# Attention with a thresholded softmax and a softplus MLP on one core: whole softmax weights for eight units instead of four, the last keys' transposes in the score banks, later sums of value halves, and keys a tile sooner

## The chip, the cores and the metric

The kernel runs on one core of a Trainium2 chip. The metric is its device time in microseconds (us); the time before is the median of three runs. Five engines work side by side, each through its own instructions in order: PE (matmuls; its weight loads show as PEld), DVE, ACT, POOL and SP, which here issues the DMAs.

## The reference

```
scores = (1/8) q k^T                       # 8 batches, 8 heads, 576 rows, 64 wide
scores = where(scores >= max(scores) - tau, scores, -1e9)
attn   = exp(scores - max) / (sum + 1e-9)
x      = (attn v), heads side by side      # 4608 tokens of 512
h      = x @ w_in                          # 512 -> 2048
out    = softplus(h) @ w_out               # 2048 -> 512
```

## The kernel before, in words

**Units and tiles.** A unit is two heads of one batch: 32 units. Each has nine tiles of 128 query rows: four of the first head's first 512 rows, one (tile 4) with the last 64 rows of both heads, four of the second head. The main loop (lines 972 to 1012) runs over 288 tiles and writes the instructions of several stages in each: the maximum and exponentials of the tile two ahead, the mask of the next, the transposes of this one, the scores of the tile three ahead, and MLP matmuls by a quota (`PAT`, one letter a step). Twice a tile `point()` runs what `defer(n, f)` put off by n points.

**A tile.** `scores` (line 443) puts 128 x 576 scores as two halves of 288 columns into one of two score buffers of two PSUM banks each; the rest of each bank is free. `row_max` (DVE, negm), `exps` (ACT, into e_all, then thr) and `mask` (DVE: scores compared with thr, times e_all, row sums kept) follow. The next scores into that buffer wait for the mask.

**Whole and halved weights.** For a unit with `s.whole` (the first `NF`) the fp32 weights are transposed on PE: `whole_T` (line 492) makes four 128 x 128 transposes into a PSUM tile tm and a fifth of 64 columns, the last keys', into another, tr; `whole_copy` lets ACT copy both to SBUF (gw); `whole_values` multiplies with fp32 values in 20 products a unit, and ACT copies the result to xp. For the others `weights_hi` (POOL) and `weights_lo` (DVE) split the weights into two f16 halves e16, a transposing DMA on SP brings them to eT (`weights_T`), values are scaled (ACT) and split in two (POOL, `split_v`, tile vt), and `values` (line 561) makes 36 f16 products a unit. A product then holds both value halves in its partitions; `values_out` copies one half to xp on ACT and adds the other on DVE.

**Keys and queries.** `load` fetches k and q of the unit after next (SP), `split_k` and `split_q` split them on POOL, `qkT` transposes them on PE, ACT copies them out, and two DMAs (`swap`, lines 425 and 426) exchange the partition halves of the queries, since scores need both arrangements. `ST` gives the tile of the unit before at which each of these eight steps stands (`pre`, line 895; `extras`, line 907), `VO` the tiles at which the four products of halved values stand, counted on into the next unit.

**The MLP.** Chunks of 512 tokens: `hidden` (line 677), softplus on ACT in pairs with a table load, halves on POOL (g), `project` (line 741). The first chunk starts at tile 42, in unit 4. The weights are prepared by ACT, POOL and DVE in the first some 70 tiles, one piece in two tiles. A last part, after the attention, is the MLP alone. Score buffers apart, all PSUM tiles (h, o, pv, tr, tm, rT, topv) take turns in four banks, ps_g.

**Who sets the order.** Tile's scheduler orders each engine's instructions from the order of writing; from tile 72 on (`TQ`) DVE and ACT keep the order of writing. All of it is fixed before the run.

Of the kernel before, what the change touches and what calls it, by code (L numbers as in the profile page):

```python
# [9 lines left out]
F32 = mybir.dt.float32  # L10
# [4 lines left out]
ALU = mybir.AluOpType  # L15
# [9 lines left out]
P = 128  # L25
# [7 lines left out]
LAG0 = 6  # L33
PAT = "RemhlTfpSfxvwp"
WD = 4
ST = (1, 3, 4, 4, 5, 6, 6, 8)
VO = (7, 8, 11, 12)
RT = 1
Q9 = (0.9, 1.1, 0.9, 1.1, 1.1, 0.8, 1.2, 0.6, 1.1)
WS2 = 2  # L40
LT = 4
WB = 3
NW = 33
NF = 4
NX = 5
TE = 84
VW = (2, 5, 7, 9)
# [14 lines left out]
def tile_kernel(ctx: ExitStack, tc: tile.TileContext, q, k, v, tau, w_in, w_out, out):  # L62
# [13 lines left out]
    SR = S - SM  # L76
    HS = S // 2
    NC = SM // P
# [12 lines left out]
    ps_g = ctx.enter_context(tc.tile_pool(name="ps_g", bufs=GB, space=PSUM))  # L91
# [66 lines left out]
    vec = Queue(nc.vector)  # L158
# [148 lines left out]
    units = []  # L307
    for b in range(B):
        for hp in range(NPAIR):
            s = Unit()  # L310
            s.i, s.b, s.hp = len(units), b, hp
            s.whole = s.i < NF
            s.r_d = dpool.tile([9, P], F32, name=f"r_d{s.i}")
            units.append(s)

    def load(s):
        h0 = 2 * s.hp
        s.kn = apool.tile([P, 10, D], F32, tag="nat", bufs=2, name=f"kn_{s.i}")
        s.qn = apool.tile([P, 10, D], F32, tag="nat", bufs=2, name=f"qn_{s.i}")
        for t, src in ((s.kn, k), (s.qn, q)):  # L320
            load_rows(s, t, src)
            for j in range(2):
                nc.sync.dma_start(t[j * SR:(j + 1) * SR, NC, :], src[s.b, h0 + j, SM:S, :])
# [119 lines left out]
    def scores(s, t):  # L443
        if t == 0:
            s.sums = apool.tile([P, 9], F32, tag="sums", name=f"sums_{s.i}")
            s.e, s.sp, s.m, s.e16, s.eT = {}, {}, {}, {}, {}
        sp = banks[nth[0] % SB]
        s.e[t] = e_all[:, nth[0] % EB, :]
        nth[0] += 1
        s.sp[t] = sp  # L450
        if t == M:
            parts = [(qm[:, n, j, :], j) for j in range(2) for n in range(2)]
        else:
            j, c = divmod(t, NC + 1)
            parts = [(s.qT[j][n][:, c * P:(c + 1) * P], j) for n in range(2)]
        for m, (lhs, j) in enumerate(parts):
            for hf in range(2):
                nc.tensor.matmul(sp[:, hf, 0:HS], lhs, s.kT[j][:, hf * HS:(hf + 1) * HS],  # L458
                                 start=(m == 0), stop=(m == len(parts) - 1))
# [32 lines left out]
    def whole_T(s, t):  # L492
        e = s.e.pop(t)
        main = ps_g.tile([P, NC, P], F32, tag="g", name=f"tm_{s.i}_{t}")
        rest = ps_g.tile([P, NC, P], F32, tag="g", name=f"tr_{s.i}_{t}")[0:SR, 0, :]
        for c in range(NC):
            nc.tensor.transpose(main[:, c, :], e[:, SR + c * P:SR + (c + 1) * P], ident)
        nc.tensor.transpose(rest, e[:, 0:SR], ident)
        s.e16[t] = main, rest
# [61 lines left out]
    def values(s, g):  # L561
        if g == 0:
            s.xp = apool.tile([P, S], F32, tag="xp", bufs=NX, name=f"xp_{s.i}")
        j, x0 = g // 2, g % 2 * HS
        o = ps_g.tile([P, 512], F32, tag="g", name=f"pv_{s.i}_{g}")
        for c in range(9):
            slot = 0 if c == 0 else 1 + 4 * ((c - 1) % 2) + (c - 1) // 2
            nc.tensor.matmul(o[:, 0:HS], s.vt[:, j, slot, :], s.eT[j][:, c, x0:x0 + HS], start=(c == 0), stop=(c == 8))  # L568
        defer(1, lambda: values_out(s, g, o))

    def values_out(s, g, o):
        j, x0, n = g // 2, g % 2 * HS, HS
        keep = slice(j * D, (j + 1) * D)
        move = slice((1 - j) * D, (2 - j) * D)
        xs = s.xp[keep, x0:x0 + n]
        act.copy(xs, o[move, 0:n])
        vec.tensor_tensor(out=xs, in0=o[keep, 0:n], in1=xs, op=ALU.add)

    def row_scales(s):
        s.rs = apool.tile([P, 9], F32, tag="rs", name=f"rs_{s.i}")  # L580
        if s.whole:
            vec.tensor_scalar(out=s.rs, in0=s.sums, scalar1=1e-9, scalar2=None, op0=ALU.add)
        else:
            vec.tensor_scalar(out=s.rs, in0=s.sums, scalar1=1e-9, scalar2=v_scale[:, s.i:s.i + 1],
                              op0=ALU.add, op1=ALU.mult)
        vec.reciprocal(s.rs, s.rs)

    def row_scales_T(s):
        ps = ps_g.tile([P, 512], F32, tag="g", name=f"rT_{s.i}")
        nc.tensor.transpose(ps[0:9, 0:P], s.rs, ident)  # L590
        defer(1, lambda: row_scales_out(s, ps))
# [255 lines left out]
    def defer(n, f):  # L847
        if n == 0:
            f()
        else:  # L850
            later.append((now["p"] + n, f))
# [38 lines left out]
    for kind, g in WL:  # L890
        for m in range(4):
            n = len(prep)
            prep.append((int(W0 + n * W1), prep_w, (kind, g, m)))

    def pre(s, first_):

        def a():
            split_k(s)
        def b():
            split_q(s, 0)  # L900
            qkT(s, 0, 0)
        def d():
            split_q(s, 1)
        return [a, b, lambda: qkT(s, 0, 2), lambda: qkT(s, 0, 1), d, lambda: qkT(s, 1, 0), lambda: qkT(s, 1, 1),
                lambda: qkT(s, 1, 2)]

    def extras(i, t):

        cur = units[i]
        nxt = units[i + 1] if i + 1 < len(units) else None  # L910
        prev = units[i - 1] if i else None
        for s, t_ in ((prev, t + 9), (cur, t)):
            if s and t_ in (VW if s.whole else VO):
                (whole_values if s.whole else values)(s, (VW if s.whole else VO).index(t_))
        if t == RT and prev:
            row_scales_T(prev)
        if t == 8:
            row_scales(cur)
        if nxt:
            if t == 0:  # L920
                cur.nxt = pre(nxt, False)
            for n, f in enumerate(cur.nxt):
                if ST[n] == t:
                    f()
        for f in plan.pop((i, t), ()):
            f()
        if t == 8 and i + 2 < len(units):
            load(units[i + 2])

    plan = {}  # L930
# [26 lines left out]
    for n in (0, 2, 1):  # L957
        qkT(u0, 1, n)
        point()
    u0.eng, u0.eng_lo = eng, nc.gpsimd  # L960
    scores(*tiles[0])
    row_max(*tiles[0])
    exps(*tiles[0])
    scores(*tiles[1])
    row_max(*tiles[1])
    exps(*tiles[1])
    mask(*tiles[0])
    scores(*tiles[2])
    load_v(units[1])

    done = 0.0
    for g, (cur, t) in enumerate(tiles):
# [7 lines left out]
        for step in PAT:  # L980
            if step == "T":
                if cur.whole:
                    whole_T(cur, t)
                    whole_copy(cur, t)
                else:
                    weights_T(cur, t)
            elif step == "h" and nxt and not nxt[0].whole:
                weights_hi(*nxt)
            elif step == "l" and not cur.whole:
                weights_lo(cur, t)  # L990
            elif step == "R" and ahead:
                row_max(*ahead)
            elif step == "e" and ahead:
                exps(*ahead)
            elif step == "m" and nxt:
                mask(*nxt)
            elif step == "f":
                upto += quota / PAT.count("f")
                while done < upto:
                    done += next(ffn)  # L1000
            elif step == "x":
                extras(cur.i, t)
            elif step == "S" and g + 3 < NS:
                scores(*tiles[g + 3])
            elif step == "v":
                slow_products()
            elif step == "w":
                while prep and prep[0][0] <= g:
                    _, f, a = prep.pop(0)
                    f(*a)  # L1010
            elif step == "p":
                point()

    last = units[-1]
    rest = {15: lambda: row_scales_T(last), 21: lambda: values(last, 2), 24: lambda: values(last, 3)}
# [36 lines left out]
```

## Time and profile before

| | |
|---|---|
| runs, median (lowest to highest) | 1436.69 us (1435.36 to 1439.61) |
| the profiled execution, its time | 1435.47 us |
| its span in the trace | 1433.2 us |
| mean granted clock of PE | 0.967 |
| PE busy | 1267.3 us (88%), 6996 matmuls |
| POOL busy | 1010.3 us (70%) |
| DVE busy | 948.6 us (66%) |
| ACT busy | 901.3 us (63%) |

Busy times are sums of instructions' durations; a busy PE overlaps the end of one matmul with the next, so its sum is no measure of its pace. A group of the profile reads: line, engine, operation, output<-input, shapes, count, then busy time and mean ns of one, then the engine's idle time just before them and what ended it. Most DVE and ACT work has line 151, a helper's, so its groups are told apart by names. A row of the waits reads: who waited <- for whom: us in all, times, longest.

### The profile page before, as it was taken

How to read it: one execution, taken by the hardware profiler on the slowest of the kernel's cores; microseconds unless marked ns; L12 is line 12 of the kernel's file. 1: busy time of each engine (PE TensorE's matmuls, PEld its weight loads, DVE VectorE, ACT ScalarE, POOL GpSimd, SP SyncE). 2: the span in 40 equal slices, each digit the busy share in tenths (PEclk: the TensorE clock that was granted, in tenths of full speed). 3: DMA queues.
4: the chain of work that ended last, by engine and by line, in shares of the span. 5: the costliest groups of instructions: out<-in, count | busy, mean ns of one | idle time of the engine just before them, and what ended most of it. 6: DMA issues, size and time to landing. Idle time of an engine off the chain costs nothing.

```text
span 1433.2 us, 21979 instructions
## 1 busy us (share of the span) xinstructions
PE 1267.3 (88%) x6996; PEld 741.0 (52%) x6996; DVE 948.6 (66%) x1747; ACT 901.3 (63%) x1683; POOL 1010.3 (70%) x1085
## 2 busy tenths in 40 slices
PE   6988477878899989999999999999989899999998
PEld 5555244444555555555555545555555655554455
DVE  6788777876777776778677877777567575651011
ACT  5777475755576658766876677666765658653222
POOL 2678999888777777778777877787766667546242
PEclk9999689989999999999999999999999999999999
DMA  5544566745766676667666666666547545541010
GB/s 152 140 131 114 125 148 152 146 98 114 157 120 132 133 154 131 135 133 156 132 132 130 141 144 128 130 134 157 126 95 155 112 105 107 97 78 39 1 37 15
DMA packets 395074, 170.83 MB, mean 119 GB/s; under 512 B 337072, under 2 KB 374224, under 8 KB 394960
## 3 DMA queue, kind: packets, MB, share of 16 engines
q1 hardware_dynamic: 394960, 169.45, 54.3%
q8 instruction: 55, 0.90, 0.3%
q14 instruction: 59, 0.48, 0.1%
HBM read 63.96 MB, written 10.63 MB: 52 GB/s over the span
## 4 chain that ended last, share of the span: by engine, by line
PE 35%; ACT 20%; DVE 15%; POOL 12%; DMA 8%; issue 7%; SPq 3%; DVEq 0%; ACTq 0%; POOLq 0%
PE o L754 12%; PE h L690 8%; PE s L458 6%; ACT st L151 6%; ACT L151 5%; DVE negm L151 5%; DMA qT<-qT 4%; PE pv L568 4%; ACT e_all L151 3%; DVE e L151 3%; DVE e_all L151 3%; ACT xp L151 2%; PE pv L527 2%; POOL e L541 1%; PE tr L405 1%
## 5 line engine op out<-in xcount | busy, mean ns | idle before, releaser
L754 PE MATMUL o<-w_o,g 128*128 128x512 f16 x1728 | 425.2, 386 | 7.3 <-ACT kT L151 4.8
L690 PE MATMUL h<-xh,w_i 128*128 128x512 f16 (+1 forms) x1280 | 368.2, 363 | 11.7 <-ACT kT L151 6.8
L541 POOL TENSOR_SCALAR e<-e_all 128x576 f16<-128x576 f32 x252 | 229.1, 911 | 159.8 <-DVE e_all L151 155.7
L151 ACT ACTIVATE e_all<-s,negm 128x576 f32<-128x576 f32 x288 | 213.4, 741 | 180.8 <-DVE negm L151 167.9
L458 PE MATMUL s<-kT,qT 128*128 128x288 f32 x1024 | 224.1, 337 | 96.8 <-DVE e_all L151 53.4
L690 PEld LDWEIGHTS <-w_i 128*128 128x128 f16 x1920 | 179.9, 99 | 173.6 <-issue 22.5
L151 DVE TENSOR_REDUCE negm<-s 128x1 f32<-128x576 f32 x288 | 215.8, 750 | 66.0 <-PE s L458 63.6
L754 PEld LDWEIGHTS <-g 128*128 128x128 f16 x1728 | 158.7, 99 | 176.3 <-issue 13.9
L458 PEld LDWEIGHTS s<-kT,qT 128*128 128x128 f32 x1024 | 156.9, 197 | 175.6 <-DVE e_all L151 115.6
L151 DVE SCALAR_TENSOR_TENSOR e_all<-s,thr,e_all 128x576 f32<-128x576 f32 x288 | 232.8, 808 | 20.5 <-ACT thr L151 18.8
L151 DVE SCALAR_TENSOR_TENSOR e<-e_all,e 128x576 f16<-128x576 f32 x252 | 233.5, 926 | 19.5 <-POOL e L541 19.3
L690 PE MATMUL h<-xl,w_i 128*128 128x512 f16 (+1 forms) x640 | 232.0, 363 | 3.6 <-POOL xl L175 3.6
L174 POOL TENSOR_SCALAR g<-st 128x512 f16<-128x512 f32 x144 | 91.6, 638 | 138.1 <-ACT st L151 137.7
L175 POOL TENSOR_TENSOR g<-st,g 128x512 f16<-128x512 f32 x144 | 176.1, 1225 | 9.3
L151 DVE TENSOR_TENSOR xp<-pv,xp 64x288 f32<-64x288 f32 x112 | 50.5, 451 | 184.7 <-ACT xp L151 184.1
L151 DVE SCALAR_TENSOR_TENSOR acc<-o,c,acc 128x512 f32<-128x512 f32 x108 | 80.1, 742 | 132.5 <-PE o L754 71.7
L151 ACT ACT_TABLE_LOAD x119 | 152.7, 1283 | 24.0 <-DVE negm L151 22.3
L568 PE MATMUL pv<-eT,vt 128*128 128x288 f16 x1008 | 151.1, 291 | 0.0
L151 ACT ACTIVATE st<-h,c 128x512 f32<-128x512 f32 x144 | 91.2, 684 | 71.1 <-PE h L690 70.4
L568 PEld LDWEIGHTS <-vt 128*128 128x128 f16 x1008 | 97.0, 100 | 46.6 <-issue 4.2
L151 ACT COPY xp<-pv 64x288 f32<-64x288 f32 (+3 forms) x132 | 50.6, 386 | 92.2 <-PE pv L568 88.3
L151 ACT ACTIVATE st<-st,c 128x512 f32<-128x512 f32 x144 | 96.0, 714 | 2.1
(104 smaller groups left out, 1561.5 us busy)
## 6 DMA issues: line engine op xcount, KB each, us to landing
qT<-qT SPq DMA_DIRECT2D x124, 128.0 KB
vn<-in_v_dram SPq DMA_DIRECT2D x112, 128.0 KB
kn<-in_k_dram SPq DMA_DIRECT2D x32, 256.0 KB
qn<-in_q_dram SPq DMA_DIRECT2D x32, 256.0 KB
wc_i<-in_moe_w_in_dram SPq DMA_DIRECT2D x16, 512.0 KB
R<-r_d SPq DMA_DIRECT2D x64, 128.0 KB
wc_o<-in_moe_w_out_dram SPq DMA_DIRECT2D x16, 512.0 KB
out_dram<-acc SPq DMA_DIRECT2D x32, 256.0 KB
```

What stands on the lines that cost most here:

```text
L151: i = getattr(self.eng, name)(*args, **kwargs)
L174: nc.gpsimd.tensor_scalar(out=hi, in0=x, scalar1=1.0, scalar2=1.0, op0=ALU.mult, op1=ALU.mult)
L175: nc.gpsimd.tensor_tensor(out=lo, in0=x, in1=hi, op=ALU.subtract)
L405: nc.tensor.transpose(pr[:, c * P:(c + 1) * P], src, identr)
L458: nc.tensor.matmul(sp[:, hf, 0:HS], lhs, s.kT[j][:, hf * HS:(hf + 1) * HS], start=(m == 0), stop=(m == len(parts) - 1))
L527: nc.tensor.matmul(o[0:D, 0:n], s.vn[k_, 5 * j + c, :], h[k_, c, 0:n], start=(c == 0), stop=(c == NC))
L541: nc.gpsimd.tensor_scalar(out=h[:, :, 0, :], in0=s.e[t].rearrange("p (c n) -> p c n", n=SR), scalar1=2.0 ** 15, scalar2=1.0, op0=ALU.mult, ...
L568: nc.tensor.matmul(o[:, 0:HS], s.vt[:, j, slot, :], s.eT[j][:, c, x0:x0 + HS], start=(c == 0), stop=(c == 8))
L690: nc.tensor.matmul(bank[:, i * u.T:(i + 1) * u.T], wi[g, cc][:, a, e], x[cc], start=(cc == 0 and m == 0), stop=(cc == NCC - 1 and m == 2))
L754: nc.tensor.matmul(o, u.g[fc][m // 2][:, sl], wo[fc][:, m % 2, :], start=(n == 0), stop=(n == 3 * QF - 1))
```

## The change

- `NF` 4 -> 8: units 4 to 7 keep weights and values whole, as units 0 to 3 do.
- The fifth transpose goes to columns 288 to 415 of the first bank of the score buffer that the same tile's scores were in, not to a PSUM tile of its own; by then that buffer holds the scores of the tile two later.
- The DVE sum of value halves is put off by one point behind ACT's copy.
- `ST`: six of the eight steps that prepare the next unit's keys and queries stand a tile sooner. `VO`: the products of halved values stand a tile sooner. The loads for the unit after next are issued at tile 7 instead of 8.

```diff
-ST = (1, 3, 4, 4, 5, 6, 6, 8)
-VO = (7, 8, 11, 12)
+ST = (0, 2, 3, 3, 4, 5, 6, 8)
+VO = (6, 7, 10, 11)
...
-NF = 4
+NF = 8
...
     def scores(s, t):
...
         s.sp[t] = sp
+        s.bank[t] = sp
...
     def whole_T(s, t):
         e = s.e.pop(t)
         main = ps_g.tile([P, NC, P], F32, tag="g", name=f"tm_{s.i}_{t}")
-        rest = ps_g.tile([P, NC, P], F32, tag="g", name=f"tr_{s.i}_{t}")[0:SR, 0, :]
+        rest = s.bank.pop(t)[0:SR, 0, HS:HS + P]
...
     def values_out(s, g, o):
...
         act.copy(xs, o[move, 0:n])
-        vec.tensor_tensor(out=xs, in0=o[keep, 0:n], in1=xs, op=ALU.add)
+        defer(1, lambda: vec.tensor_tensor(out=xs, in0=o[keep, 0:n], in1=xs, op=ALU.add))
...
     def extras(i, t):
...
-        if t == 8 and i + 2 < len(units):
+        if t == 7 and i + 2 < len(units):
             load(units[i + 2])
```

The change moves instructions on every engine. First PE at the first tiles of unit 1 (tm the four transposes, tr or s_1 the fifth, s_0 and s_1 the two score buffers, pv value products). Before:

```order
L497 MATMUL tm_1_0_564<-identr_81,e_all_129 128x128 x3
L498 MATMUL tr_1_0_565<-identr_81,e_all_129 64x128 [waits Activation_49]
L458 MATMUL s_0_130<-kT_1_0_350,qT0_1_0_389 128x288 [waits DVE_49]
L458 MATMUL s_0_130<-kT_1_0_350,qT0_1_0_389 128x288
L458 MATMUL s_0_130<-kT_1_0_350,qT1_1_0_390 128x288 x2
L527 MATMUL pv_0_3_578<-gw_0_3_500,vn_0_171 64x256 [waits Activation_49]
```

After:

```order
L498 MATMUL tm_1_0_555<-identr_81,e_all_129 128x128 x3
L528 MATMUL pv_0_3_568<-gw_0_3_492,vn_0_171 64x256 [waits Activation_49]
L528 MATMUL pv_0_3_568<-gw_0_3_492,vn_0_171 64x256
L499 MATMUL s_1_131<-identr_81,e_all_129 64x128 [waits Activation_49]
L459 MATMUL s_0_130<-kT_1_0_321,qT0_1_0_356 128x288 [waits DVE_49]
L459 MATMUL s_0_130<-kT_1_0_321,qT0_1_0_356 128x288
L459 MATMUL s_0_130<-kT_1_0_321,qT1_1_0_357 128x288 x2
```

The fifth transpose (line 499) has moved behind value products, into buffer s_1; the ACT instruction that it waits for is the exponentials of tile 2, whose scores are in s_1. In all 72 whole tiles the mask of the tile two later (DVE) waits for ACT's copy of that transpose; before it waited for thr.

Then SP, where the swapped queries of unit 14 are issued (qn_15 the query load of the unit after; qm the last rows' queries, qT the others'; eT a transposing DMA). Before:

```order
L556 DMA_TRANSPOSE eT_13_1_5869<-e16_13_4_5801 128x9x64
L630 DMA xst_6_0_11937<-x_d0_93 128x256
L425 DMA qm_95<-qm_95 64x256
L426 DMA qm_95<-qm_95 64x256
L425 DMA qT1_14_0_5901<-qT0_14_0_5900 64x512
L426 DMA qT1_14_0_5901<-qT0_14_0_5900 64x512
L559 DMA_TRANSPOSE eT_13_1_5869<-e16_13_5_5866 128x9x128
L326 DMA qn_15_6089<-in_q_dram 128x2x256
```

After:

```order
L557 DMA_TRANSPOSE eT_13_1_5891<-e16_13_4_5826 128x9x64
L326 DMA qn_15_6057<-in_q_dram 128x2x256
L425 DMA qm_95<-qm_95 64x256
L426 DMA qm_95<-qm_95 64x256
L425 DMA qT1_14_0_5863<-qT0_14_0_5862 64x512
L426 DMA qT1_14_0_5863<-qT0_14_0_5862 64x512
L323 DMA qn_15_6057<-in_q_dram 64x64 x2
```

The query load, which waits until POOL has split unit 14's second queries, now stands ahead of the swaps; so it is in units 10 to 25.

Last DVE, at the sums of value halves of unit 12 (xp), between the maxima (negm), masks (e_all) and low halves (e16) of unit 13. Before:

```order
L151 TENSOR_TENSOR xp_12_5593<-pv_12_2_5783,xp_12_5593 64x288
L151 TENSOR_REDUCE negm_13_5_5795<-s_0_130 128x1
L151 SCALAR_TENSOR_TENSOR e_all_129,sums_13_5535<-s_1_131,thr_13_4_5754,e_all_129 128x576
L151 SCALAR_TENSOR_TENSOR e16_13_3_5759<-e_all_129,e16_13_3_5759 128x9x64
L151 TENSOR_REDUCE vtop_14_5847<-vn_14_5693 128x1
L151 TENSOR_TENSOR xp_12_5593<-pv_12_3_5828,xp_12_5593 64x288
```

After:

```order
L151 TENSOR_TENSOR xp_12_5561<-pv_12_2_5744,xp_12_5561 64x288
L151 TENSOR_REDUCE negm_13_5_5820<-s_0_130 128x1
L151 SCALAR_TENSOR_TENSOR e_all_129,sums_13_5546<-s_1_131,thr_13_4_5769,e_all_129 128x576
L151 SCALAR_TENSOR_TENSOR e16_13_3_5774<-e_all_129,e16_13_3_5774 128x9x64
L151 TENSOR_TENSOR xp_12_5561<-pv_12_3_5799,xp_12_5561 64x288
L151 TENSOR_REDUCE vtop_14_5864<-vn_14_5700 128x1
```

The adds stand where they stood, or one instruction sooner, while on PE the products they add stand a tile sooner.

More of the change, by code (lines that the diff above doesn't have):

```diff
@@ L445, in scores @@
             s.sums = apool.tile([P, 9], F32, tag="sums", name=f"sums_{s.i}")
-            s.e, s.sp, s.m, s.e16, s.eT = {}, {}, {}, {}, {}
+            s.e, s.sp, s.m, s.e16, s.eT, s.bank = {}, {}, {}, {}, {}, {}
         sp = banks[nth[0] % SB]
```

## The prediction

> **What bounds the kernel now.** I read the page's head first, then one table of stretches cut at the units (a unit is two heads of one batch, nine tiles of 128 query rows), then the waits of PE in two of these stretches. Columns of the table: length, then busy time (x instructions) of PE, PEld, DVE, ACT, POOL, granted clock, DMA share, GB/s.
>
> ```profile
> span 1433.2 us, 21979 instructions
> 13.00:133.20 120.20, 103.28 (x566) 69.34 (x566) 96.74 (x208) 89.23 (x229) 76.14 (x82) 0.96 0.49 137
> 133.20:182.50 49.30, 27.99 (x124) 17.27 (x122) 38.44 (x58) 24.96 (x52) 45.37 (x47) 0.72 0.50 120
> 133.20:334.50 201.30, 144.03 (x715) 83.62 (x714) 156.22 (x268) 120.55 (x221) 178.02 (x185) 0.86 0.59 133
> 334.50:1275.00 940.50, 861.57 (x4875) 503.57 (x4874) 661.38 (x1213) 636.36 (x1143) 688.99 (x735) 0.99 0.62 129
> 412.50:449.40 36.90, 34.39 (x196) 19.73 (x194) 25.80 (x47) 26.90 (x51) 26.25 (x30) 1.00 0.68 132
> 1275.00:1433.20 158.20, 153.07 (x820) 79.97 (x817) 28.65 (x53) 49.84 (x80) 63.81 (x75) 1.00 0.11 29
> ```
>
> There are four stages. Units 0 to 3 (13.0 to 133.2) take 30.1 us each. Units 4 to 7 (133.2 to 334.5) take 50.3 us each with POOL busy 178.0 of 201.3 us and DVE 156.2, while PE does 144.0 at a clock of 0.86: the vector engines bound this stage. From unit 8 on a unit takes 36.9 us (the row at 412.5) and PE is 93% busy at full clock: PE bounds, and each of its waits costs its length. The tail is the MLP alone, at 97% PE; the change doesn't touch it.
>
> Waits of PE, first from 334.5 to 1275, then from 133 to 334.5 (us, times, longest), and between them the longest wait of any engine in the first stretch:
>
> ```profile
> PE s L458 <- DMA qT<-qT: 33.5, 22, 3.5
> PE s L458 <- DVE e_all L151: 21.1, 40, 3.1
> PE tr L405 <- DVE topv L151: 9.1, 12, 0.8
> DVE xp L151 <- ACT xp L151: 180.0, 80, 6.8
> PE s L458 <- DVE e_all L151: 35.6, 20, 9.7
> ```
>
> So in the long stage PE loses 33.5 us where the first scores of the next unit wait for the swapped queries, and 21.1 us where scores wait for a mask. DVE stands 180 us before the sum of value halves, but DVE is only 70% busy there; that wait counts only as far as masks behind it are late.
>
> **Units 4 to 7: what goes.** Groups of the stretch 133.2 to 334.5 alone, by form:
>
> ```profile
> L541 POOL TENSOR_SCALAR e<-e_all 128x576 f16<-128x576 f32 x35 | 30.4, 868 | 6.9 <-DVE e_all L151 6.2
> L151 DVE SCALAR_TENSOR_TENSOR e<-e_all,e 128x576 f16<-128x576 f32 x35 | 38.0, 1087 | 11.0 <-POOL e L541 11.0
> L175 POOL TENSOR_TENSOR vt<-vn,vt 128x576 f16<-128x576 f32 x8 | 11.4, 1422 | 0.5
> L174 POOL TENSOR_SCALAR vt<-vn 128x576 f16<-128x576 f32 x8 | 7.7, 959 | 0.2
> L151 ACT ACTIVATE vn<-vn,v_scale 128x576 f32<-128x576 f32 x8 | 6.2, 771 | 0.0
> L151 DVE TENSOR_TENSOR xp<-pv,xp 64x288 f32<-64x288 f32 x12 | 5.4, 452 | 0.2
> ```
>
> Whole weights need no f16 halves, no split values, no sums of halves. POOL loses 30.4 + 11.4 + 7.7 = 49.5 us of its 178.0; DVE loses 38.0 + 5.4 = 43.4 of 156.2, and the 11.0 it stood waiting for POOL. On SP 40 transposing DMAs and 12 of the 24 value loads go too; nothing in this stage waits on them long, so I count them at nothing.
>
> **Units 4 to 7: what comes.** From units 0 to 3, which already work so: PE's timeline (start, length), beside it nine products of f16 halves in a later unit, and ACT's groups of the whole run:
>
> ```profile
> 84.75 0.66 PE L497 MATMUL tm<-identr,e_all 128*128 128x128 f32 x4
> 85.24 0.27 PE L498 MATMUL tr<-identr,e_all 128*64 128x128 f32 x1
> 85.27 0.54 PE L405 MATMUL tr<-identr,k 128*128 128x128 f32 x4
> 85.74 1.22 PE L527 MATMUL pv<-gw,vn 128*64 128x256 f32 x4
> 86.89 0.80 PE L458 MATMUL s<-kT,qT 128*128 128x288 f32 x4
> 502.80 0.60 PE L754 MATMUL o<-w_o,g 128*128 128x512 f16 x2
> 503.24 1.27 PE L568 MATMUL pv<-eT,vt 128*128 128x288 f16 x9
> 504.35 1.03 PE L754 MATMUL o<-w_o,g 128*128 128x512 f16 x4
> L151 ACT COPY gw<-tm 128x512 f32<-128x512 f32 x32 | 18.6, 582 | 8.1 <-PE tm L497 8.0
> L151 ACT COPY gw<-tr 64x128 f32<-64x128 f32 x32 | 8.4, 263 | 0.0
> ```
>
> Matmuls overlap, so I price them from start to start. Five transposes take 85.27 - 84.75 = 0.52 us, 4.7 a unit. A value product of whole weights takes (86.89 - 85.74) / 4 = 0.29 us, 20 a unit = 5.8; nine of f16 halves take 504.35 - 503.24 = 1.11, four times 4.4. PE gains 4.7 + 5.8 - 4.4 = 6.1 us a unit. ACT gains about 36 x (0.58 + 0.26) = 30 us of copies and loses 6.2 of scaling: 120.6 + 24 = 145. (Value copies stay about as they are.)
>
> With POOL at 128.5 and DVE at 113, PE paces the stage: 36.9 + 6.1 = 43.0 us for units 5 to 7, 129 in all. Unit 4 has MLP work only in its last three tiles; its POOL falls from 45.4 to 33 of 49.3 us, and I put it at 42. That is 171 for 201.3: **-30 us**. The bounds: PE's 144.0 us at the later stage's clock are 144.0 x 0.86 / 0.99 = 125, with the added 24 us 149, and at its 93% 161 us; if ACT, in order and at 145, waits for transposes as long as POOL now works, 196. So -40 to -5.
>
> **The last keys' transposes in score banks (units 0 to 7).** The order shows what this does: before, the fifth transpose of a tile follows its four; now it stands behind the exponentials of the tile two later, whose scores lie in that bank, and the mask of that tile now waits until ACT has copied the transposes out. Transpose and copies become links of the chain scores, maximum, exponentials, mask, next scores. Two tiles of unit 1, ACT and DVE:
>
> ```profile
> 49.99 0.74 ACT L151 ACTIVATE e_all<-s,negm 128x576 f32<-128x576 f32 x1
> 51.51 0.81 DVE L151 SCALAR_TENSOR_TENSOR e_all<-s,thr,e_all 128x576 f32<-128x576 f32 x1
> 54.57 0.74 ACT L151 ACTIVATE e_all<-s,negm 128x576 f32<-128x576 f32 x1
> 57.60 0.81 DVE L151 SCALAR_TENSOR_TENSOR e_all<-s,thr,e_all 128x576 f32<-128x576 f32 x1
> ```
>
> The links are 0.27 + 0.58 + 0.26 = 1.11 us behind the exponentials. In the first tile the mask starts 51.51 - 50.73 = 0.78 us after them, in the second 57.60 - 55.31 = 2.29: the first would be 0.3 late, the second not at all. Fully on the path it costs 1.11 us x 72 = 80, fully hidden nothing; I take 0.25 us a tile, since DVE, busy 97 of 120 us there, has other work to put between: **+18 us**. One PSUM buffer fewer per tile is worth nothing by these rows (no wait of PE for it above).
>
> The Trainium skill speaks against this edit: its page "PSUM — Partial Sum Buffer", section "PSUM bank collisions raise a hardware error", has two engines keep apart by bank and partition quadrant, not by address. Hence the wait, though the columns differ. The trace of before has no such sharing and can't show it.
>
> **Keys a tile sooner.** At one unit's end, on PE:
>
> ```profile
> 515.51 0.53 PE L405 MATMUL tr<-identr,q 128*128 128x128 f32 x4
> ...
> 520.50 0.50 PE L458 MATMUL s<-kT,qT 128*128 128x288 f32 x2
> 520.84 0.23 PE L405 MATMUL tr<-identr,q 128*128 128x128 f32 x1
> 523.09 0.53 PE L458 MATMUL s<-kT,qT 128*128 128x288 f32 x2 [2.03 <-DMA qT<-qT]
> ```
>
> From the query transposes to the swapped halves' landing it takes 523.09 - 515.51 = 7.6 us (ACT's copy, SP's queue, the DMA); PE had 5.5 us of other work. In the new order 28 f16 products (0.22 each: 502.80 to 503.24 for two, above) and ten score parts (0.17 each: 520.50 to 520.84 for two) stand between: 7.9 us. That covers 7.6, barely. But the loads also move, and in units 10 to 25 the next unit's query load now stands ahead of the swaps on SP, waiting for POOL's two passes over the second queries:
>
> ```profile
> L124 POOL TENSOR_SCALAR q<-qn 128x256 fp32r<-128x256 f32 x31 | 15.0, 485 | 10.3 <-PE tr L405 10.3
> L131 POOL TENSOR_TENSOR q<-qn,q 128x256 fp32r<-128x256 f32 x31 | 30.1, 971 | 2.3
> L151 ACT ACTIVATE qT<-tr,qscale 128x512 fp32r<-128x512 f32 x64 | 44.3, 692 | 22.2 <-PE tr L405 22.2
> ```
>
> They take 1.46 us against the 0.69 of ACT's copy, and POOL may come to them late. So the path is 7.6 to some 9 us against 7.9, and the mean wait of 33.5 / 22 = 1.5 falls to 0 to 0.9. I take 70% off: -23.5 us (bounds -13 to -33.5).
>
> **Sums of halves later, values a tile sooner.** DVE's queue keeps the adds where they were, but product and ACT copy come earlier, so most of the 180 us goes. On the path: a quarter of the 21.1 us of late masks, -5 (0 to -15), and half of topv's 9.1, -4.5, since the transposes leave that place. Against it, a value bank is held until the later add; PE now finds one product and the next transposes behind it. If one in seven of the 96 adds in this stage holds PE for its 0.45 us, that is +6 (one in two: +20). The stage: -23.5 - 5 - 4.5 + 6 = **-27 us**.
>
> **The sum.** -30 + 18 - 27 = -39. The profiled execution took 1435.5 us (2.3 outside its span), 1.2 under the median 1436.7: 1436.7 - 39 = 1398 us.
>
> **Rivals.**
> - The PSUM chain decides (slower). For it: DVE is in order, and a mask that waits for ACT holds everything behind it; ACT's softplus pairs can stand ahead of the copies. Against: many masks already start over 1.1 us after the exponentials. At the full 1.11 us: -30 + 80 - 27 = +23, 1460 us. It decides from (30 + 27) / 72 = 0.79 us a tile. Chance 0.15. This is where the Trainium skill's bank rule, above, would lead.
> - SP's order eats the keys' gain: the query waits stay, -30 + 18 - 3.5 = -15.5, 1421 us. For it: 7.9 us of cover against up to 9. Chance 0.15.
> - Units 4 to 7 change engine, not pace (ACT and PE as late as POOL was): -5 + 18 - 27 = -14, 1423 us. Chance 0.17.
> - All covers hold: units 4 to 7 run as dense and at the clock of the later ones, 161 us, -40; the chain costs nothing; the later stage gains 33.5 + 10 = 43.5. 1436.7 - 83.5 = 1353 us. Chance 0.13. The Trainium skill's page "TensorE: Matmul & The Clock Gate", section "Part 1: The HAM clock gate", says that PE drops to half rate after some 3.4 us idle; the clock of 0.72 beside waits of up to 9.7 us agrees.
>
> The forecast has 0.40. The range leaves out most of the first and the last rival: 1360 to 1440 us. A measurement tells 0.3%, 4 us, from no change. Faster: 0.38 from the forecast, 0.13 from the last rival, 0.26 from the two middle ones = 0.77; slower 0.17 (the chain, and a little of the middle ones); within 0.3%: 0.06.
>
> **What would show it.** Right: the stretch of units 4 to 7 near 180 us with POOL under 75% and a clock over 0.9; PE's wait for the qT DMA under 15 us; DVE's wait for ACT's xp under 60. Units 0 to 3 longer by 5 to 15 us, with DVE e_all waiting for ACT gw. Wrong: units 0 to 3 over 150 us (the chain), the qT wait still over 25 (SP's order), units 4 to 7 over 195.

## The result and the profile after

Three runs of the changed kernel took 1409.71, 1416.19 and 1421.86 us, against a median of 1436.03 us before; a fourth, at 7199.22 us, was disturbed by something that no trace here shows and is left out. The ratio, with its 95% interval, is 0.9857 [0.9825, 0.9889]: about 20 us faster, where 39 were forecast. The forecast of 1398 was 18 us below the median of the three, and its range (1360 to 1440) holds the result.

The profiled execution took 1409.71 us. The head of its page, and the table of stretches cut at the first maximum of units 0, 4, 8 and 25 and at the last one (columns as in the prediction: length, then busy time and instructions of PE, PEld, DVE, ACT, POOL, granted clock, DMA share, GB/s):

```profile
span 1407.9 us, 22132 instructions
```

```profile
13.10:135.90 122.80, 101.25 (x565) 67.10 (x566) 100.57 (x201) 91.61 (x231) 79.89 (x87) 0.99 0.49 138
135.90:311.20 175.30, 167.38 (x872) 97.90 (x871) 107.35 (x222) 133.66 (x287) 115.70 (x125) 0.97 0.31 84
311.20:966.60 655.40, 595.41 (x3291) 350.27 (x3290) 480.16 (x858) 435.88 (x803) 474.01 (x516) 0.97 0.64 132
966.60:1248.20 281.60, 272.56 (x1621) 168.44 (x1620) 199.06 (x355) 199.91 (x349) 203.96 (x222) 0.99 0.58 123
1248.20:1407.90 159.70, 154.09 (x823) 80.17 (x821) 27.18 (x52) 50.06 (x80) 65.30 (x77) 1.00 0.11 29
```

The long stage of before (units 8 to 31) has to be split the same way, since its two parts went opposite ways:

```profile
334.50:972.00 637.50, 581.72 (x3260) 336.16 (x3259) 470.50 (x860) 435.69 (x794) 482.28 (x513) 0.99 0.65 136
972.00:1275.30 303.30, 280.14 (x1620) 167.53 (x1619) 191.18 (x353) 200.94 (x350) 206.71 (x222) 0.98 0.54 115
```

Units 0 to 3 are 2.7 us longer (122.8 for 120.1, counted from 13.1 in both). Units 4 to 7 are 26.0 shorter, with POOL busy 66% and a clock of 0.97. Units 25 to 31 are 21.7 shorter. But units 8 to 24 are **17.9 us longer**, and their clock fell from 0.99 to 0.97. The tail is 1.8 longer (159.7 for 157.9, counted from 1275.3). Together that is the 25.3 us by which the span shrank.

What changed in units 8 to 24 shows in the waits (us, times, longest). PE, after:

```profile
PE s L459 <- DVE e_all L151: 19.7, 16, 2.7
PE s L459 <- DMA qT<-qT: 16.4, 12, 1.9
PE o L755 <- POOL g L175: 11.3, 17, 1.2
PE h L691 <- DVE xp L151: 6.3, 2, 5.3
```

PE, before:

```profile
PE s L458 <- DMA qT<-qT: 25.3, 17, 3.2
PE s L458 <- DVE e_all L151: 15.9, 28, 3.1
```

POOL, after and then before:

```profile
POOL e L542 <- DVE e_all L151: 66.7, 39, 3.1
POOL xp L610 <- DMA R<-r_d: 64.5, 14, 7.3
```

```profile
POOL xp L609 <- DMA R<-r_d: 2.6, 1, 2.6
```

The wait for the swapped queries fell by 9 us only, and PE waits for POOL's MLP halves (g), which did not show before. Behind that stands a wait that no rival named: POOL's scaling of the attention output (xp times R) stands 64.5 us before R, the row scales that make a round trip through DRAM.

In the first two stages, DVE's masks and the fifth transposes of after show the chain through the score banks. The rows are DVE's in units 0 to 3 and in 4 to 7, and PE's in units 0 to 3.

```profile
DVE e_all L151 <- ACT gw L151: 4.3, 7, 1.0
DVE e_all L151 <- ACT gw L151: 25.8, 17, 4.8
PE s L499 <- ACT e_all L151: 8.2, 7, 3.1
```

### The profile page after: what moved, and what is told of

It reads as the page before. It is cut to its first block, busy times and chain, and to the rows that moved or that the text cites. A ratio compares the mean times of both kernels' runs of the same rounds, so it can differ in the third digit from the quotient of the medians.

```text
span 1407.9 us, 22132 instructions
## 1 busy us (share of the span) xinstructions
PE 1296.3 (92%) x7192; PEld 768.5 (55%) x7192; DVE 920.2 (65%) x1695; ACT 916.9 (65%) x1759; POOL 942.0 (67%) x1033
## 4 chain that ended last, share of the span: by engine, by line
PE 44%; POOL 15%; ACT 11%; DVE 11%; DMA 9%; issue 7%; SPq 3%; POOLq 0%; ACTq 0%; DVEq 0%
PE o L755 14%; PE h L691 13%; PE s L459 6%; PE pv L569 4%; ACT st L151 3%; ACT L151 3%; PE pv L528 3%; DVE e_all L151 3%; DVE negm L151 2%; DMA R<-r_d 2%; DMA r_d<-rt 2%; DVE e L151 2%; DMA qT<-qT 2%; ACT e_all L151 2%; POOL g L175 2%
## 5 line engine op out<-in xcount | busy, mean ns | idle before, releaser
L755 PE MATMUL o<-w_o,g 128*128 128x512 f16 x1728 | 430.2, 387 | 14.8 <-POOL g L175 12.1
L542 POOL TENSOR_SCALAR e<-e_all 128x576 f16<-128x576 f32 x216 | 195.6, 908 | 113.6 <-DVE e_all L151 108.6
L151 DVE SCALAR_TENSOR_TENSOR e<-e_all,e 128x576 f16<-128x576 f32 x216 | 213.9, 990 | 43.2 <-POOL e L542 43.0
L459 PEld LDWEIGHTS s<-kT,qT 128*128 128x128 f32 x1024 | 162.4, 196 | 100.8 <-DVE e_all L151 58.8
L175 POOL TENSOR_TENSOR g<-st,g 128x512 f16<-128x512 f32 x144 | 170.7, 1188 | 9.1
L174 POOL TENSOR_SCALAR g<-st 128x512 f16<-128x512 f32 x144 | 98.6, 687 | 106.2 <-ACT st L151 97.9
L569 PE MATMUL pv<-eT,vt 128*128 128x288 f16 x864 | 127.9, 293 | 0.0
L610 POOL TENSOR_TENSOR xp<-xp,R 128x576 f32<-128x576 f32 x32 | 45.8, 1432 | 109.2 <-DMA R<-r_d 92.6
L569 PEld LDWEIGHTS <-vt 128*128 128x128 f16 x864 | 85.9, 101 | 42.8 <-issue 4.1
L528 PE MATMUL pv<-gw,vn 128*64 128x256 f32 (+3 forms) x320 | 98.0, 423 | 0.3 <-DVE topv L151 0.3
```

The source lines that it names most:

```text
L151: i = getattr(self.eng, name)(*args, **kwargs)
L174: nc.gpsimd.tensor_scalar(out=hi, in0=x, scalar1=1.0, scalar2=1.0, op0=ALU.mult, op1=ALU.mult)
L175: nc.gpsimd.tensor_tensor(out=lo, in0=x, in1=hi, op=ALU.subtract)
L528: nc.tensor.matmul(o[0:D, 0:n], s.vn[k_, 5 * j + c, :], h[k_, c, 0:n], start=(c == 0), stop=(c == NC))
L542: nc.gpsimd.tensor_scalar(out=h[:, :, 0, :], in0=s.e[t].rearrange("p (c n) -> p c n", n=SR), scalar1=2.0 ** 15, scalar2=1.0, op0=ALU.mult, ...
L610: nc.gpsimd.tensor_tensor(out=s.xp, in0=s.xp, in1=s.R, op=ALU.mult)
```

## The experiments

Twelve kernels, four to a chip, each timed against the kernel before on its own chip. Differences are taken between ratios, times 1436 us. Stage lengths (us) are those of one profiled execution each, cut as in the table of stretches:

```
kernel        units 0-3   4-7    8-24  25-31   ratio [95%]
before          120.1   201.3   637.5  303.3   1
after           122.8   175.3   655.4  281.6   0.9857 [0.9825, 0.9889]
e7_vo_old       124.6   173.8   620.1  277.5   0.9577 [0.9549, 0.9605]
e8_rt0          125.7   180.1   622.0  278.3   0.9640 [0.9612, 0.9669]
e9_sp_order     126.7   173.8   660.1  283.0   0.9873 [0.9846, 0.9900]
e11_rt0_sp      125.0   181.6   622.9  279.5   0.9614 [0.9585, 0.9643]
f1_nodefer      124.6   175.2   640.2  291.8   0.9792 [0.9770, 0.9813]
f2_nf4          125.4   192.7   621.5  278.7   0.9713 [0.9690, 0.9735]
f3_rest_g       118.4   181.1   617.8  277.8   0.9549 [0.9529, 0.9569]
f4_oldkeys      132.2   174.7   609.1  278.2   0.9555 [0.9524, 0.9585]
g1_defer_only   119.3   197.2   609.9  281.1   0.9605 [0.9568, 0.9642]
e6_keysonly     117.6   197.1   641.4  291.0   0.9882 [0.9850, 0.9913]
g2_defer_nf8    119.9   180.4   607.7  279.9   0.9486 [0.9453, 0.9518]
g3_bank_late    121.3   180.3   604.8  278.6   0.9478 [0.9445, 0.9511]
```

### Why units 8 to 24 grew: row scales or SP's order

The theory: value products a tile sooner (`VO`) set the scaling of xp ahead of its R. The rival was the prediction's: the query load, now ahead of the swaps on SP, holds the queries. Four kernels test them.

**e7_vo_old**: the changed kernel with the value products where they were. (`XD`, the tiles by which the scaling follows, must then be 6, since it has to be written behind the last deferred sum.)

```diff
-XD = 5
+XD = 6
...
-VO = (6, 7, 10, 11)
+VO = (7, 8, 11, 12)
```

> The changed kernel with the products of halved values where they stood before, VO = (7, 8, 11, 12); XD = 6, since the sums now come half a tile later and the scaling of xp must follow them. In the built order rT is ahead of the third value product again, POOL's scaling is behind the MLP's halves, and the query load is behind the swaps. Theory R: POOL's wait for R is under 10 us in units 8 to 24, and the kernel takes 10 to 20 us less than the changed one: 0.972 to 0.979. If the sooner products were what gained in units 25 to 31 (282 us against 303), it is 0.99 or more.

**e8_rt0**: the changed kernel with the row scales' transposes a tile sooner (`XD` 7, so that the scaling is written where it was; POOL's order around it stays as in the changed kernel).

```diff
-XD = 5
+XD = 7
...
-RT = 1
+RT = 0
```

> The changed kernel with the transposes of the row scales (rT on PE) a tile sooner, RT = 0, and XD = 7, so that POOL's scaling of xp is written where it was. Theory R: in units 8 to 24 the changed kernel loses time (655 us where before took 638) because rT now stands behind a value product on PE, the scales' round trip through DRAM ends some 3 us later, and POOL, whose scaling of xp has moved ahead of the MLP's halves, stands 64.5 us there waiting for R (2.6 before). Then POOL's wait for R falls below 20 us in these units and the kernel takes about 12 us less than the changed one, ratio to before 0.977. Theory S (SP's order: the query load ahead of the swaps) expects no change: 0.986, and PE's wait for the qT DMA still about 16 us.

**e9_sp_order**: the changed kernel, with each query load put behind the swaps of the unit before in SP's order (the lines that set the order; `ds` holds the loads, `swaps` the swaps).

```diff
...
+            if src is q:
+                for d in ds:
+                    behind(d, swaps[:-1])
...
```

> The changed kernel with the three loads of the next unit's queries kept behind the swaps of this one's first queries on SP; nothing else. Theory S: PE's wait for the qT DMA in units 8 to 24 (16.4 us in the changed kernel) falls to under 3 us and the kernel takes 13 to 16 us less, ratio to before 0.976. Theory R: the qT wait falls too, but POOL's wait for R stays over 50 us, scores then wait for masks instead, and under 6 us are gained: 0.982 to 0.986.

**e11_rt0_sp**: both of these edits together.

> Both edits: row scales a tile sooner and the query loads behind the swaps. If the two causes add, 25 us less than the changed kernel, ratio to before about 0.968, units 8 to 24 in about 625 us. If the one only hides the other, no better than the better of the two alone, 0.976.

Units 8 to 24 of e7, e8 and e9, each with POOL's wait for R (e9's with PE's wait for the queries too):

```profile
311.50:931.60 620.10, 579.45 (x3295) 343.25 (x3294) 484.36 (x858) 436.41 (x803) 481.68 (x514) 0.99 0.68 139
```

```profile
POOL xp L610 <- DMA R<-r_d: 1.1, 1, 1.1
```

```profile
318.80:940.80 622.00, 580.92 (x3293) 345.95 (x3292) 473.81 (x858) 436.98 (x803) 480.24 (x515) 0.99 0.67 139
```

```profile
POOL xp L610 <- DMA R<-r_d: 23.6, 10, 4.6
```

```profile
POOL xp L615 <- DMA R<-r_d: 76.8, 14, 7.9
```

```profile
PE s L464 <- DMA qT<-qT: 11.0, 11, 1.7
```

With old value products POOL's wait for R is gone (1.1 us), units 8 to 24 are 35 us shorter and the whole 40 us. That alone does not decide, since in e7 the query load has gone back behind the swaps too. R a tile sooner, with POOL's order unchanged, cuts the wait from 64.5 to 23.6 us and wins back 31 of the 40. The forced SP order took PE's query wait from 16.4 to 11.0 us, but the R wait rose to 76.8 and nothing was gained. In e11 it added nothing that can be told from e8. So the row scales are the cause, and SP's order is not. Both e7 and e8 gained more than was expected of them (10 to 20 and about 12 us): the theory counted only the 17.9 us that the stage had lost against before, and not what the later sums, below, would have gained there.

How it comes about can be seen in unit 15. It starts at 600.8 us in before and at 582.0 in after. The transposes of the row scales (rT) on PE, before and then after, where they now stand behind a value product:

```profile
614.88 0.27 PE L590 MATMUL rT<-identr,rs 128*9 128x128 f32 x1
```

```profile
598.56 1.27 PE L569 MATMUL pv<-eT,vt 128*128 128x288 f16 x9
599.66 0.27 PE L591 MATMUL rT<-identr,rs 128*9 128x128 f32 x1
```

That is 14.1 us into the unit before and 17.7 after. On POOL meanwhile, the scaling moved the other way. Its order in unit 13 of before, then of after:

```
L174 TENSOR_SCALAR g_2_2_5849<-st_2_5814 128x512
L175 TENSOR_TENSOR g_2_2_5850<-st_2_5814,g_2_2_5849 128x512
L174 TENSOR_SCALAR g_2_3_5853<-st_3_5812 128x512
L609 TENSOR_TENSOR xp_5593<-xp_5593,R_5769 128x576
L175 TENSOR_TENSOR g_2_3_5854<-st_3_5812,g_2_3_5853 128x512
```

```
L610 TENSOR_TENSOR xp_5561<-xp_5561,R_5785 128x576
L542 TENSOR_SCALAR e_13_5_5888<-e_all 128x9x64
L124 TENSOR_SCALAR q_14_1_5914<-qn_5621 128x4x64
L131 TENSOR_TENSOR q_14_1_5914<-qn_5621,q_14_1_5914 128x4x64
L174 TENSOR_SCALAR g_2_2_5866<-st_2_5840 128x512
```

The scaling follows the values, and it came to stand ahead of two MLP halves (g) and of the next queries (q). That `VO` moved it is read from these orders: in the traces of e6 and f1, with old value products and `XD` 5 and 6, it stands right between instructions of halves in three units of four, as in before; in after it does so in none. POOL and PE of after, in unit 15:

```profile
610.76 1.40 POOL L610 TENSOR_TENSOR xp<-xp,R 128x576 f32<-128x576 f32 x1 [6.37 <-DMA R<-r_d]
612.13 0.67 POOL L542 TENSOR_SCALAR e<-e_all 128x576 f16<-128x576 f32 x1
612.76 0.40 POOL L124 TENSOR_SCALAR q<-qn 128x256 fp32r<-128x256 f32 x1
613.25 0.73 POOL L131 TENSOR_TENSOR q<-qn,q 128x256 fp32r<-128x256 f32 x1
613.94 1.70 POOL L174 TENSOR_SCALAR g<-st 128x512 f16<-128x512 f32 x2
```

```profile
616.82 0.82 PE L755 MATMUL o<-w_o,g 128*128 128x512 f16 x3 [1.09 <-POOL g L175]
620.52 0.85 PE L459 MATMUL s<-kT,qT 128*128 128x288 f32 x2 [1.93 <-DMA qT<-qT]
623.32 2.37 PE L569 MATMUL pv<-eT,vt 128*128 128x288 f16 x9
```

POOL stands 6.37 us before R and has queries and halves behind it; PE then runs out of both. With POOL on time, in e7, the query wait has left PE's list of units 8 to 24. SP's order is not the reason: in f1 and e6, below, the query load stands ahead of the swaps as in after, POOL waits for R for under 2 us, and neither list of PE's waits has a query wait. So most of what after still shows of it comes by way of POOL.

### Which part gained

**f1_nodefer**: e7 with the sum of value halves directly behind ACT's copy again, `XD` kept at 6.

```diff
-        defer(1, lambda: vec.tensor_tensor(out=xs, in0=o[keep, 0:n], in1=xs, op=ALU.add))
+        vec.tensor_tensor(out=xs, in0=o[keep, 0:n], in1=xs, op=ALU.add)
```

> From the kernel with the products where they were (ratio 0.958), the put-off of the sums of value halves undone: DVE adds at the same point as ACT copies. If the later sums gain nothing by themselves, 0.956 to 0.962 with DVE's wait for ACT's xp back from 26.9 to over 120 us in units 8 to 24 and PE's waits for masks as before. If DVE's standing there made masks late, 10 us or more are lost: 0.965 or more. In this build the query load stands ahead of the swaps again in units 10 to 25, so a qT wait could come back with it.

Without the deferral the time is 31 us longer, and the query wait that could have come back with SP's order did not. **g1_defer_only** is the kernel before with that line alone (the same line deferred, and `XD` 6).

> The kernel before with one part of the change alone: the sums of value halves put off by a point (XD = 6, so that the scaling of xp follows the last sum). Theory D: DVE's standing before these sums was what held the masks, and PE paid for it at its weight loads too (PEld waits 58 us for masks in units 8 to 24 of the kernel before, 27 us in the build with old keys): 45 to 53 us are gained, ratio 0.963 to 0.969. If the later sums pay only together with whole weights or sooner keys: 0.985 or more. The prediction's terms for this part (5 and 4.5 us gained, 6 lost) would give 0.997.

That is the ratio 0.9605 [0.9568, 0.9642]: this one line gains 57 us, more than was expected (45 to 53) and nearly three times what the whole change did. `XD` has no part in it that can be seen: f1 with 6 and e6 below with 5 agree to 1.2 us in units 8 to 24 and 0.8 in 25 to 31. Waits of units 8 to 31, of before (DVE's longest one, for ACT's xp, is in the prediction: 180.0 us):

```profile
DVE negm L151 <- PE s L458: 56.8, 51, 3.3
ACT e_all L151 <- DVE negm L151: 135.7, 104, 3.4
PEld s L458 <- DVE e_all L151: 76.2, 145, 3.4
```

The same of g1:

```profile
DVE xp L151 <- ACT xp L151: 32.9, 32, 2.2
DVE negm L151 <- PE s L458: 98.2, 103, 5.1
ACT e_all L151 <- DVE negm L151: 52.6, 29, 4.3
PEld s L458 <- DVE e_all L151: 35.1, 50, 2.0
PE s L458 <- DVE e_all L151: 13.7, 20, 1.5
PE s L458 <- DMA qT<-qT: 22.3, 17, 3.1
```

Before, DVE and ACT went in step: DVE's add waited for ACT's copy, the next maximum stood behind the add, ACT's next exponentials waited for that maximum (135.7 us) and PE for the mask at the end of it. With the add one point later DVE's wait falls from 180.0 to 32.9 and ACT's to 52.6, and DVE waits for PE instead (98.2). The price of this to PE can't be read from the 21.1 us of matmul rows in which scores waited for masks, which fall by 7.4 only. The stretch of units 8 to 31 is 49.6 us shorter. PE's idle time gives 29.5 of that (940.5 - 861.6 = 78.9 before, 49.4 in g1): beside the masks, the wait for queries falls from 33.5 to 22.3, and that of key and query transposes for topv from 9.1 to nothing. The other 20.1 are busy time (861.6 before, 841.5 in g1) for as many instructions. The weight loads' rows for masks fall by 41.1 in the same stretch; that late weights stretched the matmuls' busy time fits this but is not shown.

**e6_keysonly**: the kernel before with the new `ST` and the loads at tile 7.

```diff
-ST = (1, 3, 4, 4, 5, 6, 6, 8)
+ST = (0, 2, 3, 3, 4, 5, 6, 8)
...
-        if t == 8 and i + 2 < len(units):
+        if t == 7 and i + 2 < len(units):
```

> The kernel before with ST and the loads of the changed kernel, nothing else. The prediction priced the sooner keys at 23.5 us: 0.984, with PE's wait for the qT DMA under 15 us in units 8 to 31. If that wait was a place where a late DVE and ACT showed, the time is spent elsewhere and the ratio is 0.995 to 1.005.

**f4_oldkeys**: e7 with these two edits undone.

> From the same kernel, ST and the tile of the loads back to what they were. If the sooner keys end the qT wait, PE's wait for the qT DMA is back at 25 to 34 us in units 8 to 31 and 20 to 30 us are lost: 0.972 to 0.979. If the waits were only moved (masks instead), under 8 us are lost: 0.958 to 0.963.

PE's waits in units 8 to 31 of e6, and of f4:

```profile
PE s L458 <- DVE e_all L151: 24.3, 44, 2.4
PE h L690 <- DVE acc L151: 14.7, 8, 3.5
PE h L690 <- ACT qm L151: 13.1, 12, 1.2
```

```profile
PE s L459 <- DMA qT<-qT: 20.5, 18, 3.6
PE s L459 <- DVE e_all L151: 10.0, 17, 1.1
```

Alone, sooner keys gain 17 us, and PE's query wait leaves the list in e6; but other waits take its place, and units 8 to 24 are no shorter than before. The gain is in units 25 to 31 (291.0 for 303.3) and 0 to 7. Beside later sums they gain nothing: f4, with its query wait of 20.5 us, is as fast as e7 (0.9555 [0.9524, 0.9585] and 0.9577 [0.9549, 0.9605]). It takes 7.6 us more in units 0 to 3 and 11.0 less in units 8 to 24.

**f2_nf4**: e7 with `NF` 4.

> From the same kernel, NF back to 4: units 4 to 7 with f16 halves. If whole weights bring the gain of that stage (201.3 to 174 us), it goes back to 195 to 202 and the ratio to 0.974 to 0.978. If half of it came from earlier keys and later sums, the stage stays under 190: 0.968 or less.

**g2_defer_nf8**: g1 with `NF` 8, the fifth transposes in PSUM tiles of their own.

> The kernel before with later sums (XD = 6) and NF = 8, without the score banks, the sooner keys and the sooner products. If the parts add as the undone ones say (later sums 50 us, whole weights 19), 0.947 to 0.953. If the score banks are needed for units 4 to 7 with old keys, that stage takes over 185 us and the ratio is 0.956 or more.

Whole weights in units 4 to 7 are worth 20 us in f2 against e7 (192.7 against 173.8 in that stage) and 17 in g2 against g1 (197.2 against 180.4). That is less than the 26.0 by which the stage shrank: f2, without them, still takes 192.7 there against 201.3 before, by the other parts of the change.

**f3_rest_g**: e7 with the fifth transposes back in PSUM tiles of their own.

```diff
-        rest = s.bank.pop(t)[0:SR, 0, HS:HS + P]
+        rest = ps_g.tile([P, NC, P], F32, tag="g", name=f"tr_{s.i}_{t}")[0:SR, 0, :]
```

> From the same kernel, the last keys' transposes back in a PSUM tile of their own, for all eight whole units. If the added links in the chain of scores cost what units 0 to 3 show (120.1 us before, 124.6 in this kernel), units 0 to 3 fall back by 4 to 5 us, and units 4 to 7 by about as much unless PE there waits for the four shared banks. Chain alone: 0.952. Banks short in units 4 to 7: that stage over 178 us and 0.958 or more.

Its first two stages, to be compared with e7's below them:

```profile
13.10:131.50 118.40, 103.54 (x553) 68.51 (x554) 94.02 (x199) 86.90 (x226) 75.12 (x81) 0.94 0.51 143
131.50:312.60 181.10, 169.39 (x882) 97.20 (x881) 111.43 (x224) 135.47 (x292) 119.54 (x130) 0.98 0.30 82
```

```profile
137.70:311.50 173.80, 165.82 (x872) 96.80 (x871) 107.26 (x222) 133.59 (x287) 115.79 (x125) 0.98 0.32 85
```

Score banks cost 6.2 us in units 0 to 3 (124.6 against 118.4), and the whole table bears that out: 122.8 to 132.2 us with them, 117.6 to 121.3 without. In units 4 to 7 e7 is 7.3 us shorter than f3, but the sign is not sure: of the kernels with whole weights there, those with score banks take 173.8 to 181.6, the two without 180.4 and 181.1. In the whole time e7 and f3 can't be told apart (0.9577 [0.9549, 0.9605] and 0.9549 [0.9529, 0.9569]). The last kernel keeps score banks only in units 4 to 7, with the old keys. **g3_bank_late**: f4, with score banks from unit 4 on.

```diff
+        if s.i < 4:
+            rest = ps_g.tile([P, NC, P], F32, tag="g", name=f"tr_{s.i}_{t}")[0:SR, 0, :]
+        else:
+            rest = s.bank.pop(t)[0:SR, 0, HS:HS + P]
```

> The build with later sums, old keys and old products, with the last keys' transposes in a PSUM tile of their own in units 0 to 3 and in the score banks in units 4 to 7. Units 0 to 3 took 118 us with the first and 125 to 132 with the second, units 4 to 7 181 against 175: if each stage keeps its better number, 1355 to 1360 us, 0.945 to 0.949, the fastest of all. If the two only trade the same time (the stage after waits for the one before), 0.953 or more.

It is the fastest, 1360.58 us, 0.9478 [0.9445, 0.9511], but not told from g2, 0.9486 [0.9453, 0.9518]. Its ratio is the expected one, but not by the road expected: units 4 to 7 take 180.3 us, as without score banks, and not 175. Both beat the kernel before and the changed one, and g2 has nothing of the change but whole weights in units 4 to 7 and later sums.

## Why the prediction was right, and where it was not

That the time fell in the range is in part luck: two errors of one stage, each larger than the change measured, nearly cancelled. Of the signs that it named, units 4 to 7 came as said (175.3 us, POOL 66%, clock 0.97), and DVE's wait for ACT's xp fell to 42.8 us in units 8 to 31, where under 60 was named. PE's query wait stayed at 16.4 (under 15 was named), and units 0 to 3 grew by 2.7 us (5 to 15 were named).

- **Units 4 to 7, -30.** The stage came out as said: -26.0 with the chain in it, PE at 95% of it, so that PE paces it. Whole weights by themselves are worth less than the term, -17 to -20 by the experiments; the rest came with other parts of the change.
- **Score banks, +18.** The wait is there as described, but its size was too high: +2.7 us in units 0 to 3 as a whole, +6.2 by f3, and no sure cost in units 4 to 7. DVE's wait for the copies came to 4.3 us in units 0 to 3 and 25.8 in units 4 to 7, where DVE is busy 61% and can afford it. The program keeps to the bank rule of the Trainium skill that the prediction named ("PSUM — Partial Sum Buffer", the section "PSUM bank collisions raise a hardware error"), and the trace shows the wait that comes of it: PE's row of 8.2 us, where transposes wait for exponentials of other columns. In the whole time no price of it can be told (f3 against e7). The slower rival fell with it.
- **Keys a tile sooner, -23.5.** The step that failed is "each of its waits costs its length". The wait itself behaved about as said: 33.5 to 16.4 us in the changed kernel, none in e6. But the time went into other waits: alone, units 8 to 31 are 8.4 us shorter (641.4 + 291.0 against 637.5 + 303.3) and the whole 17, and beside later sums nothing is gained. The bound of -13 has a slip as well: 9 less 7.9 is 1.1 us a wait, not 0.9, which gives -9.
- **SP's order** did not eat the gain: e9, and e6, which has the new order and no query wait.
- **Later sums, -5 + 6.** The term that was mis-sized most. It measured -57 alone (-50 in the stage), -31 beside the sooner keys. The step that failed: DVE's 180.0 us "counts only as far as masks behind it are late", and that was then priced at a quarter of PE's matmul rows for masks (21.1 us). These gave 7.4 us of it in g1; the rest came as less waiting for queries and topv and as less busy time of PE, beside weight loads whose waits for masks fell from 76.2 to 35.1. The +6 for held value banks has no support: in both pairs of runs the deferral gained. The topv wait of 9.1 us, of which -4.5 was claimed, has left PE's list.
- **Values a tile sooner**, for which the prediction had no price but a share of these gains, measured about +40 (e7, which has `XD` 6 too). No rival had it. The prediction followed the moved products to DVE's adds, but not on to the scaling on POOL, nor to rT on PE.
- **The late stage, -27** in all: it measured -3.5, from about -50 of later sums (g1: 609.9 + 281.1 against 637.5 + 303.3) and most of it lost again through the row scales (e7: 620.1 + 277.5, 39 us less than after).

Open: how much of e7's gain over the changed kernel is `XD` 6 by itself, since with the new values it was not tried; and why f4's units 0 to 3 took 132.2 us. Not all gains add up: later sums gain 57 us alone and whole weights 17 beside them, and g2 has both (74); but the 17 of the sooner keys alone come to nothing beside later sums. Which waits take the place of the cured one was shown for e6 only.

## What to carry to other kernels

An in-order engine that waits for another's copy holds back everything behind it: put the dependent instruction one step later, and price it by following who waits for that engine in turn, weight loads of PE included. A step that is moved can take its consumers along: here the scaling followed its values and came to stand ahead of an operand that arrives by another road. A wait of PE is worth its length only if no other wait is ready to take its place.

## What the runs showed of the hardware

PE's clock fell without any long pause. The stretch of after in which PE ran out of work, one microsecond within it, and the stretch behind it:

```profile
616.20:620.60 4.40, 1.55 (x7) 0.69 (x7) 1.87 (x2) 4.34 (x8) 4.32 (x6) 0.84 0.67 167
619.00:620.00 1.00, 0.00 (x0) 0.00 (x0) 1.00 (x2) 0.99 (x2) 1.00 (x2) 0.57 0.90 199
620.60:624.60 4.00, 4.00 (x13) 2.04 (x14) 2.51 (x4) 0.39 (x1) 2.62 (x3) 0.50 0.79 152
```

PE was busy 1.55 of 4.40 us. Its longest wait there was 1.93 us, up to 620.52, and the clock was down before that wait was over (0.57 from 619 to 620 us). Then it ran 4 us at a clock of 0.50: nine value products took 2.37 us (the row at 623.32), against 1.27 at 598.56. Over units 8 to 24 a clock of 0.97 instead of 0.99 (the rows of after and of e7) is by estimate some 0.02 x 655 = 13 of the 35 us that e7 has less. The prediction cited the Trainium skill ("TensorE: Matmul & The Clock Gate", "Part 1: The HAM clock gate") for half rate after some 3.4 us idle. Taken as one pause, the trace goes against it: PE's waits from 615.7 us on came in pieces of 1.09, 0.29 and 1.93 us, and the clock fell within the last.

A busy PE is not a PE at its pace: in units 8 to 31 its busy time fell from 861.6 us in before, for 4875 instructions, to 569.7 + 271.8 = 841.5 in g1, for 3275 + 1624 = 4899, at a clock of 0.99 in both. These are g1's rows:

```profile
329.60:939.40 609.80, 569.72 (x3275) 342.86 (x3274) 480.95 (x860) 433.65 (x795) 483.42 (x514) 0.99 0.70 142
939.40:1220.50 281.10, 271.81 (x1624) 168.92 (x1623) 192.80 (x353) 200.71 (x351) 206.55 (x224) 0.99 0.59 124
```
